# Start of a fused attention and FFN kernel: order of the first loads, the mask by a scan, and batch 0's copies and v factors on other engines

## The chip, the core and the metric

The kernel runs on one core of one Trainium2 chip. The core has five engines with instruction queues of their own: TensorE (PE in the profile), VectorE (DVE), ScalarE (ACT), GpSimd (POOL) and SyncE (SP), and 16 DMA engines that they share. The metric is the device time of one execution in microseconds (us); of several runs the median is taken. Lower is better.

## What is computed

For 8 batches of 8 heads with 576 positions of 64 values, causal attention with a decay: the bias of query i on key j is the difference of a running sum of max(s, 0). Its output, 4608 tokens of 512 values, goes through an RMS norm and a SwiGLU FFN with 1536 hidden columns.

```python
scores = scale * np.matmul(q, k.transpose(0, 1, 3, 2))
cum = np.cumsum(np.maximum(s, 0.0), axis=-1)
bias = -(cum[:, :, :, None] - cum[:, :, None, :])
scores = np.where(causal, -1000000000.0, scores + np.minimum(bias, 0.0))
attn = softmax(scores)                       # over the keys
x = np.matmul(attn, v)                       # to [4608, 512]
xn = x / np.sqrt(np.mean(x * x, axis=-1, keepdims=True) + 1e-06) * rms_g
g = xn @ w_gate
out = (g * sigmoid(g) * (xn @ w_val)) @ w_out
```

(The last lines are put together from the reference's two functions.)

## The kernel before

**Stages.** The kernel works in nine rounds (`for c in range(NCH)`, line 823). Round c computes the FFN of 512 tokens (gate and value products in `ffn1_group`, line 721; output product in `ffn2`, line 740), and beside it prepares and computes the attention of batch c + 1. Batch 0 has no FFN to stand beside: its loads, its preparation and most of its attention (lines 768 to 815) run alone at the start. This stretch is where the change lies.

**The planner.** No order is written by hand. Each instruction is handed to the class `Plan` (line 76) with its engine, an estimated duration in us, a key (lower is more urgent), and for loads two lags and a transfer time. `schedule` (line 140) plays the program through with these estimates: for each engine it takes the most urgent instruction that would be ready, and so fixes the order of every engine's queue. On the chip each engine then works through its queue in that order, and each instruction waits for the data it needs. An estimate is thus no time on the chip, but it decides who stands ahead of whom. `R.after` adds a dependence, `R.order` only an order of starts. Where the plan has TensorE idle in the first 24 us, it fills the gap with dummy products on the tile `still`, "spins" (line 861)[...]. A GpSimd load waits until the load eight before it on that queue has landed (`LANES`, line 83).

**Loads of the start.** GpSimd issues the loads of the start, in one order (`R.order(*loads)`, line 820): K and Q of the first 256 positions of batch 0 (`kqa`), two blocks of v of 128 positions, K and Q of the other 320 positions (`kqb`, the "second part"), the other three blocks of v, then gate and value weights in three pieces each, K and Q of batch 1 in two pieces each, half of the output weights, v of batch 1, and the other half. These loads turn fp32 into bf16 for K, Q and weights; K of batch 0 lands beside Q in the tile `q_nat`, and those of batch 1 in `k_nat`.

**Constants.** `ident_bf` is a 128x128 identity in bf16 for transposes on TensorE. Before, GpSimd makes it with `make_identity` (a memset and a select) between the loads `kqa` and the first v. `tri` is a 128x128 mask: 0 where the query is not before the key, -30000 elsewhere. GpSimd makes it with a memset and a select (lines 781 to 783). TensorE adds it to batch 0's diagonal score blocks as a product of `ident_bf` and `tri`. `ident_F` is the identity in fp32, copied by VectorE (line 784).

**Decay.** `decay` (line 516) turns s into factors: max with 0, a scan over 576 positions, an exp on ScalarE, a transpose on TensorE into a PSUM tile (`wP`), and a copy of that to SBUF in bf16 (`wT`). The bias becomes a factor on each row of v: `prep_v` (line 498) multiplies a block of v by it. For batch 0 all five blocks are done by VectorE from `wP`; for later batches GpSimd does it from `wT`. A dependence puts batch 0's last three blocks behind `norms[3]`, the fourth head pair's division by the softmax sum.

**Transposes of K and Q.** `prep_transpose` (line 460) takes one of four head pairs: TensorE transposes K and Q into two PSUM banks, VectorE copies K to `KT`, ScalarE copies Q to `QT`. Batch 0 goes through it twice, part 0 for the first 256 positions and part 1 for the rest.

**Attention of batch 0.** `attention` (line 689) works in two halves of four units (a unit is a head pair): scores on TensorE (`unit_scores`), exp on ScalarE, then the product with v on TensorE (`unit_av`) and the division on VectorE. The second half needs part 1 of K and Q, all five v blocks, and also the "near" scores between the halves (`near_scores`). For each block of 128 tokens the squares are summed (`att_square`), GpSimd makes the norm's factor alpha (`att_alpha`, two instructions), VectorE or ScalarE scales, TensorE transposes, and VectorE writes `xnT` (`att_out`), which the FFN reads. The first FFN group needs `xnT` of token blocks 0 and 1 and the first pieces of both weights.

Of the kernel before, what the change touches and what calls it, by code (L numbers as in the profile page):

```python
# [270 lines left out]
def kernel(  # L271
# [12 lines left out]
    nc = tc.nc  # L284
    fp32 = mybir.dt.float32
# [3 lines left out]
    ALU = mybir.AluOpType  # L289
    AX = mybir.AxisListType  # L290

    B, H, S, D = q.shape
# [4 lines left out]
    NB = 5  # L297
# [19 lines left out]
    pers = ctx.enter_context(tc.tile_pool(name="pers", bufs=1))  # L317
# [3 lines left out]

    ident_bf = pers.tile([128, 128], bf16, name="ident_bf")
    still = pers.tile([128, 256], bf16, name="still")
    tri = pers.tile([128, 128], bf16, name="tri")
    ident_F = pers.tile([128, 128], fp32, name="ident_F")
    ident_f = ident_F[0:64, 0:64]
# [5 lines left out]
    s_all = pers.tile([BH, S], fp32, name="s_all")  # L332
# [4 lines left out]
    wT = pers.tile([128, NB, BH], bf16, name="wT")  # L337
# [38 lines left out]
    R = Plan(banks)  # L376
# [3 lines left out]
    def real(a):  # L380
        return a.get(banks) if isinstance(a, View) else a

    def I(eng, method, us, key=None, kind=None, dma=0.0, lags=(1.2, 1.2), **kw):
        outs = [kw[n] for n in ("out", "accum_out") if n in kw]
        ins = [a for n, a in kw.items()
               if n not in ("out", "accum_out") and isinstance(a, (bass.AP, View))]
        f = getattr(ENG[eng], method)
        o = R.add(eng, us, lambda: f(**{n: real(a) for n, a in kw.items()}), outs, ins, key=key,  # L388
                  lat=LAT[eng], kind=kind, dma=dma,
                  name=outs[0].bank.name if isinstance(outs[0], View) else outs[0].name)  # L390
        o.lags = lags
        return o

    def fill(eng, ap, value, us, key=None):
        f = ENG[eng].memset
        return R.add(eng, us, lambda: f(ap, value), [ap], [], key=key, lat=LAT[eng], name=ap.name)

    def mms(us, items, key=None):
        def emit():
            for out, lhsT, rhs, st, sp, tr in items:  # L400
                out = real(out)
                if tr:
                    nc.tensor.matmul(out, lhsT=lhsT, rhs=rhs, is_transpose=True, start=st, stop=sp)  # L403
                else:
                    nc.tensor.matmul(out, lhsT=lhsT, rhs=rhs, start=st, stop=sp)  # L405
        o = R.add("pe", us, emit, [i[0] for i in items],
                  [i[1] for i in items] + [i[2] for i in items], key=key, lat=0.22,
                  name=items[0][0].bank.name)
        o.n_mm = len(items)
        return o  # L410
# [8 lines left out]
    def bank(group, cap):  # L419
        return View(Bank(group, group, cap))  # L420
# [4 lines left out]
    def lay(b, dt, pattern=None, n=None, **sizes):  # L425
        a = b if dt == fp32 else b.bitcast(dt)
        a = a[:, 0:n] if n else a
        return a.rearrange(pattern, **sizes) if pattern else a


    def load_runs(b, which, h0, h1, key, part=0):
        c0, c1 = PARTS[part] if b == 0 else (0, KC)
        p0 = KP * which
        us = ((1.5, 1.6)[part] * (h1 - h0) / 8) if b == 0 else 2.85 * (h1 - h0) / 8
        return I("pool", "dma_start", 0.7, key=key, dma=us, lags=(0.95, 1.1),
                 out=raw[b][part][p0 : p0 + KP, h0:h1, :, :].rearrange("p h c d -> p h (c d)"),
                 in_=(k, q)[which][b, h0:h1, KP * c0 : KP * c1, :].rearrange(
                     "h (p c) d -> p h (c d)", c=c1 - c0))
# [7 lines left out]
    def load_rows(dst, src, b, eng, key):  # L446
        return [load_row(dst, src, b, sc, eng, key) for sc in range(NB)]
# [12 lines left out]
    def prep_transpose(b, hp, key, part=0):  # L460
        c0, c1 = PARTS[part] if b == 0 else (0, KC)
        n, t0 = c1 - c0, KP * c0
        t = [lay(bank("kq", 4), bf16, "p (c t) -> p c t", n=KP * n, c=n) for w in range(2)]
        mm = mms(0.1 + 0.025 * n if b == 0 else 0.34,
            [(t[w][64 * j : 64 * j + 64, c, :], raw[b][part][KP * w : KP * w + KP, 2 * hp + j, c, :],
              ident_bf[KP * w : KP * w + KP, KP * w : KP * w + KP], c == 0, c == n - 1, True)
             for c in range(n) for j in range(2) for w in range(2)], key=key)
        for w, dst in enumerate((KT, QT)):
            o = dst[b % 2][:, hp, t0 : t0 + KP * n].rearrange("p (t c) -> p t c", c=n)
            i = t[w].rearrange("p c t -> p t c")  # L470
            if w == 0:
                I("dve", "tensor_copy", 0.12 + 0.062 * n, key=key, out=o, in_=i)
            else:
                I("act", "activation", 0.18 + 0.045 * n, key=key, out=o, in_=i, func=AF.Copy)
        return mm
# [22 lines left out]

    def prep_v(b, sc, eng, key):
        n = 128 if sc < 4 else 64  # L500
        wb = (wP if b == 0 else wT)[0:n, sc, b * H : (b + 1) * H]
        return I(eng, "tensor_tensor", 1.0 if eng == "pool" else 0.62, key=key,
          out=vw[b % 2][0:n, sc, :, 0:64], in0=v_nat[b % len(v_nat)][0:n, sc, :, :],
          in1=wb.unsqueeze(2).to_broadcast([n, H, D]), op=ALU.mult)

    def prep_w(b, eng, key):
        for n, c0, c1 in ((128, 0, 4), (64, 4, 5)):
            o = vw[b % 2][0:n, c0:c1, :, 64:65]
            i = wT[0:n, c0:c1, b * H : (b + 1) * H].unsqueeze(3)
            if eng == "act":  # L510
                I("act", "activation", 0.25, key=key, out=o, in_=i, func=AF.Copy)
            else:
                I(eng, "tensor_copy", 0.25, key=key, out=o, in_=i)


    def decay(key):
        I("dve", "tensor_scalar", 0.5, key=key, out=s_all, in0=s_all, scalar1=0.0, scalar2=None,
          op0=ALU.max)
        I("dve", "tensor_tensor_scan", 1.3, key=key, out=cum, data0=ones[:, 0:1].to_broadcast([BH, S]), data1=s_all, initial=0.0,
          op0=ALU.mult, op1=ALU.add)  # L520
        I("dve", "tensor_scalar", 0.1, key=key, out=half, in0=cum[:, S - 1 : S], scalar1=-0.5,
          scalar2=None, op0=ALU.mult)
        I("act", "activation", 0.7, key=key, kind="exp", out=w_row[:, 0:S], in_=cum, func=AF.Exp,
          bias=half, scale=1.0)
        tp = lay(bank("w", 1), fp32, "p (c b) -> p c b", n=NB * BH, c=NB)
        mms(0.6, [(tp[:, sc, :], w_row[:, sc * 128 : (sc + 1) * 128], ident_f, sc == 0,
                   sc == NB - 1, True) for sc in range(NB)], key=key)
        I("dve", "tensor_copy", 0.42, key=key, out=wT, in_=tp)
        return tp
# [210 lines left out]
    def ffn2(c, key, step):  # L740
# [24 lines left out]
    STEP = PER / 144  # L765


    I("sp", "dma_start", 0.5, key=-100, dma=0.5, out=s_all, in_=s.rearrange("b h s -> (b h) s"))
    I("sp", "dma_start", 0.5, key=-90, dma=0.1, out=g4,
      in_=moe_rms_g.rearrange("(cc p) -> cc p", p=128))  # L770
    fill("dve", still, 0.0, 0.1, key=-101)
# [2 lines left out]
    def ident(t, key):  # L774
        R.add("pool", 0.5, lambda: make_identity(nc, t), [t], [], key=key, lat=0.06).n_pool = 2

    kqa = [load_runs(0, w, h, h + 8, -100) for h in range(0, H, 8) for w in range(2)]
    ident(ident_bf, -99.5)
    kqb = [load_runs(0, w, h, h + 8, -92, part=1) for h in (0,) for w in range(2)]
    v0 = load_rows(v_nat[0], v, 0, "pool", -94)  # L780
    R.add("pool", 0.25, lambda: nc.gpsimd.memset(tri, 0.0), [tri], [], key=-99.3, lat=0.06)
    I("pool", "affine_select", 0.35, key=-99.3, out=tri, in_=tri, pattern=[[1, 128]],
      compare_op=ALU.is_ge, fill=-30000.0, base=0, channel_multiplier=-1)
    I("dve", "tensor_copy", 0.15, key=-93.7, out=ident_F, in_=ident_bf)
    wl = []
    for i, (lo, hi) in enumerate(zip(WL, WL[1:])):
# [1 line left out]
            wl.append(load_w(w, lo * 128, hi * 128, -93 + 0.1 * i))  # L788
    dec = len(R.ops)
    wP = decay(-95)  # L790
    fills = []
    for t in KT:
        fills.append(fill("dve", t[:, :, S : NB * 128], 0.0, 0.17, key=-90))
# [10 lines left out]
    o = mms(0.1, [(gp_[:, 0:CC], g4, ident_F[0:CC, 0:CC], True, True, True)], key=-75)  # L804
    R.after(o, kqt[HP - 1])
    I("dve", "tensor_copy", 0.1, key=-75, out=g_sb, in_=gp_[:, 0:CC])
    prep_w(0, "act", -70)
    vops = [prep_v(0, sc, "dve", -70 if sc < 2 else -62) for sc in range(NB)]
    norms = attention(0, -78, 3, 4)
    for o in vops[2:]:  # L810
        R.after(o, norms[3])
# [2 lines left out]
    for o in R.ops[n0:]:  # L814
# [7 lines left out]
           in_=moe_rms_g.unsqueeze(0).to_broadcast([128, DM]))  # L822
    for c in range(NCH):
# [4 lines left out]
        b = c + 1  # L828
        if b < B:
# [12 lines left out]
            vops = [prep_v(b, sc, "pool", K - 8 + sc) for sc in range(NB)]  # L842
        if b + 1 < B:
            n = b + 1
            K2 = K - 14 + LEAD
            for sc in range(NB):
                for dst, src in ((k_nat, k), (q_nat, q)):
                    o = load_row(dst, src, n, sc, "sp", K2 + sc)
# [186 lines left out]
```

## Time and profile before

| what | us |
|---|---|
| median of 7 runs | 354.05 |
| lowest and highest of them | 352.5 and 354.64 |
| the profiled execution | 353.3 |
| its span, first to last instruction | 351.6 |
| TensorE busy in the span | 341.3 (97%) |
| K and Q of the first part: issued | 1.33 and 2.23 |
| first block of v: issued | 4.23 |
| K and Q of the second part: issued | 6.04 and 6.72 |
| first FFN product starts | 24.33 |

The profile is of one execution. Its span is shorter than its time by 1.7 us, which lie before the first and after the last instruction that the profile shows. Times within it count from the first instruction. A row of the timeline gives start, length, engine, line, operation, the tiles written and read (without their number in the ring for PSUM and for groups), and in brackets how long the engine had been idle before, and what ended it. Most instructions are recorded on lines 388, 403 and 405, the helpers that issue them, so tiles tell them apart. "POOL ... DMA_DIRECT2D" is GpSimd's work of issuing a load; the data land later. The chain of waits is followed back from the last instruction, at each step to whatever released it.

### The profile page before, as it was taken

How to read it: one execution, taken by the hardware profiler on the slowest of the kernel's cores; microseconds unless marked ns; L12 is line 12 of the kernel's file. 1: busy time of each engine (PE TensorE's matmuls, PEld its weight loads, DVE VectorE, ACT ScalarE, POOL GpSimd, SP SyncE). 2: the span in 40 equal slices, each digit the busy share in tenths (PEclk: the TensorE clock that was granted, in tenths of full speed). 3: DMA queues.
4: the chain of work that ended last, by engine and by line, in shares of the span. 5: the costliest groups of instructions: out<-in, count | busy, mean ns of one | idle time of the engine just before them, and what ended most of it. 6: DMA issues, size and time to landing. Idle time of an engine off the chain costs nothing.

```text
span 351.6 us, 8062 instructions
## 1 busy us (share of the span) xinstructions
PE 341.3 (97%) x3037; PEld 209.4 (60%) x3037; DVE 254.8 (72%) x497; ACT 228.9 (65%) x467; POOL 127.0 (36%) x201
## 2 busy tenths in 40 slices
PE   7799999999999999999999999999999999999994
PEld 5579775788479765886544554455455444444443
DVE  5878868698568994989499958996787557707730
ACT  2769999785767986857695668666988433223321
POOL 8754294501481339113921293029325100000000
PEclk9899999999999999999999999999999999999999
DMA  7999998997898886997967896777631130020012
GB/s 140 209 209 207 261 198 185 204 219 172 194 145 230 139 187 119 228 157 178 147 173 182 190 173 156 209 176 140 171 77 33 58 102 0 1 91 30 0 36 93
DMA packets 140550, 51.16 MB, mean 145 GB/s; under 512 B 127316, under 2 KB 135256, under 8 KB 140504
## 3 DMA queue, kind: packets, MB, share of 16 engines
q1 hardware_dynamic: 131832, 41.13, 52.9%
q0 software_dynamic: 8672, 9.44, 14.8%
q8 instruction: 26, 0.43, 0.5%
q14 instruction: 20, 0.16, 0.2%
HBM read 38.16 MB, written 9.44 MB: 135 GB/s over the span
## 4 chain that ended last, share of the span: by engine, by line
PE 93%; DMA 2%; POOL 1%; DVE 1%; issue 1%; ACT 0%; POOLq 0%; DVEq 0%; ACTq 0%
PE psc L405 14%; PE psb L405 12%; PE psf L405 12%; PE psd L405 11%; PE psa L405 11%; PE psg L405 11%; PE pse L405 10%; PE psh L405 10%; DMA q_nat<-in_q_dram 2%; POOL q_nat L388 1%; POOL v_nata L388 1%; PE psa L403 0%; PE psb L862 0%; PE psf L403 0%; PE psh L403 0%
## 5 line engine op out<-in xcount | busy, mean ns | idle before, releaser
L405 PEld LDWEIGHTS <-wg_sb 128*128 128x128 bf16 x624 | 60.0, 98 | 32.5 <-issue 0.4
L405 PEld LDWEIGHTS <-wv_sb 128*128 128x128 bf16 x624 | 59.7, 98 | 32.8 <-issue 1.8
L405 PEld LDWEIGHTS <-Hs 128*128 128x128 bf16 x444 | 41.1, 98 | 42.0 <-DVE Hs L388 0.2
L388 POOL TENSOR_SCALAR_AFFINE_SELECT Eb<-Eb 128x512 bf16<-128x512 bf16 x7 | 4.5, 639 | 78.5 <-ACT Eb L388 78.5
L405 PE MATMUL psc<-wout_sb,Hs 128*128 128x512 bf16 x96 | 23.7, 379 | 0.0
L388 DVE SCALAR_TENSOR_TENSOR x_blkb<-x_blkb,alb,gB 128x512 bf16<-128x512 bf16 x15 | 12.7, 892 | 11.0 <-POOL alb L388 11.0
L405 PE MATMUL psf<-xnT,wg_sb 128*128 128x256 bf16 (+1 forms) x116 | 20.6, 313 | 0.0
L388 POOL TENSOR_TENSOR vwb<-v_nata,wT 128x512 bf16<-128x512 f32 (+1 forms) x20 | 20.3, 1040 | 0.0
L388 ACT ACTIVATE sq_scr<-x_blkb 128x512 bf16<-128x512 bf16 x20 | 12.7, 633 | 10.0 <-DVE x_blkb L388 9.6
L405 PE MATMUL psb<-wout_sb,Hs 128*128 128x512 bf16 (+1 forms) x84 | 19.0, 364 | 0.0
L405 PE MATMUL psa<-xnT,wv_sb 128*128 128x256 bf16 (+1 forms) x108 | 18.6, 308 | 0.0
L388 ACT ACTIVATE sq_scr<-x_blka 128x512 bf16<-128x512 bf16 x18 | 11.4, 632 | 9.6 <-DVE x_blka L388 9.4
L405 PE MATMUL psg<-xnT,wv_sb 128*128 128x256 bf16 (+1 forms) x108 | 17.6, 300 | 0.0
L388 ACT ACTIVATE sq_scr<-q_bf 128x1024 bf16<-128x1024 bf16 (+1 forms) x18 | 16.4, 914 | 0.2
L405 PE MATMUL psd<-wout_sb,Hs 128*128 128x512 bf16 (+1 forms) x72 | 16.4, 361 | 0.0
L388 ACT ACTIVATE sq_scr<-k_bf 128x1024 bf16<-128x1024 bf16 (+1 forms) x18 | 16.3, 906 | 0.0
L388 DVE CAST k_bf<-k_nat 128x512 bf16<-128x512 f32 (+1 forms) x30 | 16.1, 537 | 0.0
L388 POOL TENSOR_TENSOR vwa<-v_nata,wT 128x512 bf16<-128x512 f32 (+1 forms) x15 | 15.4, 1052 | 1.1 <-DMA v_nata<-in_v_dram 1.0
L405 PE MATMUL psc<-xnT,wv_sb 128*128 128x256 bf16 (+1 forms) x84 | 15.5, 318 | 0.3 <-DVE u_sbc L388 0.3
L388 POOL TENSOR_SCALAR_AFFINE_SELECT Ef<-Ef 128x512 bf16<-128x512 bf16 (+1 forms) x14 | 7.1, 527 | 23.9 <-ACT Ef L388 23.9
L405 PE MATMUL psb<-xnT,wg_sb 128*128 128x256 bf16 (+1 forms) x92 | 15.5, 305 | 0.0
L388 DVE CAST q_bf<-q_nat 128x512 bf16<-128x512 f32 (+1 forms) x30 | 15.3, 510 | 0.0
(475 smaller groups left out, 874.2 us busy)
## 6 DMA issues: line engine op xcount, KB each, us to landing
v_nata<-in_v_dram SPq DMA_DIRECT2D x24, 256.0 KB, 4.2
k_nat<-in_k_dram SPq DMA_DIRECT2D x24, 256.0 KB, 3.2
q_nat<-in_q_dram SPq DMA_DIRECT2D x24, 256.0 KB, 3.7
out_dram<-osba SPq DMA_DIRECT2D x12, 256.0 KB, 2.3
out_dram<-osbb SPq DMA_DIRECT2D x12, 256.0 KB, 2.4
out_dram<-osbc SPq DMA_DIRECT2D x11, 256.0 KB, 3.0
v_nata<-in_v_dram POOLq DMA_DIRECT2D x8, 256.0 KB, 9.9
wout_sb<-in_moe_w_out_dram POOLq DMA_DIRECT2D x2, 768.0 KB, 15.8
```

Of the source, the lines that this page charges most:

```text
L388: o = R.add(eng, us, lambda: f(**{n: real(a) for n, a in kw.items()}), outs, ins, key=key, lat=LAT[eng], kind=kind, dma=dma, name=outs[0]. ...
L405: nc.tensor.matmul(out, lhsT=lhsT, rhs=rhs, start=st, stop=sp)
```

## The change

- GpSimd issues the first two v loads straight behind `kqa`. The identity's memset is now VectorE's, and its select stands behind the second v load (`R.order(v0[1], o)`).
- The mask is no longer made by GpSimd. VectorE makes it from the identity: a scan along each row, with a column of ones (`one`) as factor, gives 1 from the diagonal on and 0 before it; then subtract 1 and multiply by 30000. Both instructions are put behind the decay's `half`.
- The planner's lags for the load of s are 0.8 and 0.8 where they were 1.2 and 1.2.
- Blocks 2, 3 and 4 of batch 0's v get their factors on GpSimd, from `wT`; blocks 0 and 1 stay on VectorE, from `wP`.
- In the second part, VectorE copies Q of head pairs 2 and 3; ScalarE keeps those of 0 and 1.

```diff
@@ -321,6 +321,7 @@
     still = pers.tile([128, 256], bf16, name="still")
+    one = pers.tile([128, 1], fp32, name="one")
@@ -468,7 +469,7 @@
-            if w == 0:
+            if w == 0 or part and hp in (2,3,):
                 I("dve", "tensor_copy", 0.12 + 0.062 * n, key=key, out=o, in_=i)
             else:
                 I("act", "activation", 0.18 + 0.045 * n, key=key, out=o, in_=i, func=AF.Copy)
@@ -498,7 +499,7 @@
-        wb = (wP if b == 0 else wT)[0:n, sc, b * H : (b + 1) * H]
+        wb = (wP if eng == "dve" else wT)[0:n, sc, b * H : (b + 1) * H]
@@ -765,7 +766,7 @@
-    I("sp", "dma_start", 0.5, key=-100, dma=0.5, out=s_all, in_=s.rearrange("b h s -> (b h) s"))
+    I("sp", "dma_start", 0.5, key=-100, dma=0.5, lags=(0.8, 0.8), out=s_all, in_=s.rearrange("b h s -> (b h) s"))
@@ -775,12 +776,13 @@
     kqa = [load_runs(0, w, h, h + 8, -100) for h in range(0, H, 8) for w in range(2)]
-    ident(ident_bf, -99.5)
     kqb = [load_runs(0, w, h, h + 8, -92, part=1) for h in (0,) for w in range(2)]
     v0 = load_rows(v_nat[0], v, 0, "pool", -94)
-    R.add("pool", 0.25, lambda: nc.gpsimd.memset(tri, 0.0), [tri], [], key=-99.3, lat=0.06)
-    I("pool", "affine_select", 0.35, key=-99.3, out=tri, in_=tri, pattern=[[1, 128]],
-      compare_op=ALU.is_ge, fill=-30000.0, base=0, channel_multiplier=-1)
+    fill("dve", ident_bf, 0.0, 0.1, key=-100)
+    fill("dve", one, 1.0, 0.06, key=-100)
+    o = I("pool", "affine_select", 0.35, key=-99.5, out=ident_bf, in_=ident_bf,
+          pattern=[[-1, 128]], compare_op=ALU.not_equal, fill=1.0, base=0, channel_multiplier=1)
+    R.order(v0[1], o)
@@ -788,6 +790,13 @@
     wP = decay(-95)
+    n = len(R.ops)
+    I("dve", "tensor_tensor_scan", 0.35, key=-89, out=tri, data0=one.to_broadcast([128, 128]),
+      data1=ident_bf, initial=0.0, op0=ALU.mult, op1=ALU.add)
+    I("dve", "tensor_scalar", 0.15, key=-89, out=tri, in0=tri, scalar1=-1.0, scalar2=30000.0,
+      op0=ALU.add, op1=ALU.mult)
+    for o in R.ops[n:]:
+        R.after(o, R.ops[dec + 2])
@@ -805,7 +814,7 @@
-    vops = [prep_v(0, sc, "dve", -70 if sc < 2 else -62) for sc in range(NB)]
+    vops = [prep_v(0, sc, "dve" if sc < 2 else "pool", -70 if sc < 2 else -62) for sc in range(NB)]
```

## The prediction, made before the result was known

> **What bounds the kernel now.** I read the page first, then the chain that ended last, the timeline of the first 40 us, and stretches. The page says that TensorE is the bound over the span as a whole:
>
> ```profile
> PE 341.3 (97%) x3037; PEld 209.4 (60%) x3037; DVE 254.8 (72%) x497; ACT 228.9 (65%) x467; POOL 127.0 (36%) x201
> ```
>
> All that the change touches runs before the first FFN group, so the question is when that group starts. The chain of waits over 0 to 40 us (start, length, what) shows what comes ahead of it:
>
> ```profile
> 4.28 1.78 POOL v_nata L388 x2
> 6.06 0.67 POOL q_nat L388
> 6.72 7.59 DMA q_nat<-in_q_dram
> ...
> 17.04 1.40 PE psb L862 x6
> ...
> 23.02 0.38 PE psc L405 x12
> ...
> 24.49 0.87 PE psb L405 x8
> ```
>
> The last is the first FFN group; from there the chain is TensorE almost without a break, so a microsecond gained before 24.3 us moves the end by a microsecond, if later loads keep up. Ahead of it stands Q of the second part: issued at 6.72, landed at 14.31. GpSimd could issue it only after two v loads, and these only after it had made identity and mask (2.90 to 4.28). TensorE idles for it, and then runs at half clock (columns: busy us of each engine, granted clock, DMA share, GB/s):
>
> ```profile
> 5.14:8.55 3.41, 2.36 (x50) 1.81 (x51) 2.35 (x10) 1.16 (x2) 3.41 (x6) 1.00 1.19 235
> 11.96:15.38 3.42, 1.76 (x64) 1.28 (x62) 2.20 (x11) 1.77 (x6) 2.08 (x5) 1.00 1.16 260
> 15.38:18.79 3.41, 3.41 (x44) 2.14 (x44) 2.69 (x7) 2.20 (x6) 2.37 (x5) 0.50 1.35 203
> ```
>
> In the second part the timeline shows ScalarE as the last link: two Q copies stand among its exps, and it has two stalls of 0.8 us:
>
> ```profile
> 16.40 0.60 ACT L388 ACTIVATE Ee<-psf 128x512 bf16<-128x512 f32 x1 [0.84 <-PE psf L405]
> 17.98 0.44 ACT L388 ACTIVATE QTa<-psh 128x320 bf16<-128x320 bf16 x1
> 19.23 0.60 ACT L388 ACTIVATE Ef<-psb 128x512 bf16<-128x512 f32 x1 [0.81 <-PE psb L405]
> 20.20 0.44 ACT L388 ACTIVATE QTa<-psd 128x320 bf16<-128x320 bf16 x1
> 23.35 0.62 ACT L388 ACTIVATE Eh<-psg 128x512 bf16<-128x512 f32 x1
> ```
>
> Its last exp ends at 23.97; the last attention-times-v group starts at 23.96 to 24.00. The other feeder, xnT of token blocks 0 and 1, is ready at 22.46 + 0.67 = 23.13.
>
> [...] 0.50 for exactly 3.41 us, after a window that was 52% busy (1.76 of 3.42); after one that was 69% busy (2.36 of 3.41) it stayed full. [...] GpSimd's loads landed in the order of issue (K 6.2, Q 7.6, v 8.3 and 9.7, K 12.5, Q 14.3). So v loads issued earlier should not hold up K and Q that are ahead of them. [...] The trace shows 1.35 us for the 64x576 scan against 0.45 for the tensor_scalar of that shape.
>
> **Part 1, v loads ahead of the identity.** GpSimd spends 2.90 to 4.23 = 1.33 us on four instructions between Q's load and v. Three go away (both memsets, the mask's select); the identity's select (0.29) comes after the two v loads. So v is issued 1.33 earlier, and the second part's K and Q 1.33 - 0.29 = 1.04 earlier (Q at about 5.7). That the landing moves by as much is not given: the DMA engines are busy most of the time. What can be saved is the dip when v has drained and K has not started (0.5 us slices):
>
> ```profile
> 7.50:8.00 0.50, 0.29 (x16) 0.25 (x16) 0.00 (x0) 0.00 (x0) 0.50 (x1) 1.00 1.04 270
> 8.00:8.50 0.50, 0.50 (x17) 0.43 (x18) 0.42 (x1) 0.39 (x1) 0.50 (x2) 1.00 0.78 164
> 8.50:9.00 0.50, 0.50 (x36) 0.36 (x36) 0.48 (x2) 0.18 (x1) 0.50 (x1) 1.00 0.80 104
> 9.00:9.50 0.50, 0.50 (x20) 0.34 (x20) 0.50 (x3) 0.50 (x4) 0.50 (x2) 1.00 0.96 141
> 9.50:10.00 0.50, 0.50 (x21) 0.34 (x17) 0.42 (x2) 0.50 (x3) 0.50 (x2) 1.00 1.30 175
> ```
>
> Against a share of about 1.2 from 9.5 to 13 us, the slices 0.78, 0.80 and 0.96 lack 0.42 + 0.40 + 0.24 = 1.06; times 0.5 over 1.2 that is 0.44 us. I take **0.5**; bounds 0 [...] and 1.04. The identity is then ready at about 5.1; its first user waits for K until 6.45, so the delay is covered by 1.3 us.
>
> **Part 2, mask by scan, fills on VectorE.** Added there: memsets of the identity (0.11 to 0.17, like its neighbours) and of the column of ones (0.06), in the idle time before 3.54; the scan, by the 3-column scan at 0.12 and the 576-column one at 1.35: 0.12 + 125 x 2.15 ns = 0.39; the tensor_scalar about 0.2. ident_F's copy (0.23) moves behind the decay scan; the relu starts some 0.1 earlier. They sit behind the fills, which end at 7.3; the first K copy starts at 8.07 after an idle 0.75. 0.39 + 0.2 + 0.23 - 0.1 = 0.72 fits; overrun at most 0.2, and the first half of batch 0 has a 1.4 us wait for Q behind it (VectorE idle until 14.82). The mask's first use is at 9.06. Cost **0**. The lags of the s load alter only the planner's due times: 0.
>
> **Part 3, three v factors to GpSimd, two Q copies to VectorE.** VectorE sheds 3 x 0.68 = 2.04 us and takes 2 x 0.49 (the 128x320 K copy's price) = 0.98. ScalarE sheds the copies at 17.98 and 20.20, 2 x 0.44 busy, about 0.38 each start to start: **0.75**, on the path because its last exp is. GpSimd takes 3 x 1.04 = 3.1 us, after the fourth norm of the first half (15.9) and the v landings (16.1 and later). Queued behind them are the issues of batch 1's K and Q (17.26 to 20.87) and the alpha pair (18.58 to 19.58). Later issues cost nothing as long as the queue is fed: the weights ahead of them land as late as 16.52 + 15.9 = 32.4. The factors are needed by 22.86; three of them end at 20 to 21. But alpha feeds xnT: one factor ahead of it costs nothing, three bring xnT to about 22.9. I give back **0.3** for that.
>
> **Part 4, the half clock.** With Q 0.5 earlier, TensorE's busy time in 11.96 to 15.38 goes from 1.76 to about 2.3 (67%), near the 69% that kept the clock full. Half clock cost 0.44 on the scores (1.23 us from 15.37 against 0.79 for the same unit at 22.13) and 0.7 on the six spins (1.40 instead of 6 x 0.12). VectorE's earlier K copies bind in its place, so of 1.14 I take **0.8**, bounds 0 (window falls low again) and 1.14.
>
> **Sum.** 0.5 + 0.75 + 0.8 - 0.3 = 1.75: the first FFN group at 22.6 instead of 24.33. Does the rest keep up? The wv columns for group two land at 12.80 + 12.2 = 25.0 (24.5 shifted) and are first used at 26.95; batch 1's Q lands at 17.87 + 17.5 = 35.4 and its transposes start at 37.10. These slacks, 1.95 and 1.7, plus 0.5 cap the gain at about 2.2; at 1.75 they hold. I leave the gain at **1.7** after rounding down for new stalls. Profiled execution: 351.6 of span + 1.7 around it = 353.3; less 1.7 = 351.6. The median of the runs, 354.05, lies 0.75 above it; so **352.3**.
>
> **Rivals.** **A, the rebalancing is covered** (0.24): the planner's new order keeps TensorE waiting for copies, and only arrival and a little of the clock count, 0.7: 353.35. For it: VectorE holds K copies behind norm and square (15.48 to 16.64). Against: ScalarE really is last. **B, GpSimd becomes the bound** (0.14): all three factors ahead of alpha, or the dip only moves; gain about 1.0: 353.05. For it: GpSimd waits in order; against: alpha has the more urgent key. **C, slower** (0.13): the half clock moves instead of going. If TensorE is busy less than 52 to 69% (1.8 to 2.4 us) of the window 18.79 to 22.20, because fewer spins are planned in a shorter second part, half clock falls on 22.20 to 25.61. Then the 1.47 us of attention-times-v take 1.4 more and the FFN to 25.6 loses about 0.9, less 0.6 of arrival: +1.7, so 355.75. For it: three engines are emptier there; against: the window is 3.14 of 3.41 busy now.
>
> **Numbers.** Forecast 0.49. A measurement of this kernel can tell about 0.3% (1.06 us) from no change: faster is below 353.0, slower above 355.1. Faster: 0.45 of the forecast, 0.05 of A, 0.07 of B = 0.57; slower: C and a little of A = 0.14; same 0.29. Range: low end the 2.2 cap and scatter among runs, 351.2; high end takes in A and B with scatter, 354.7. The forecast's own range is 351.6 to 353.0.
>
> **What would show it.** Q landing near 13.8 (step 1); no copy of VectorE later than 8.3 for the scan (2); ScalarE without the copies at 18 and 20 and alpha before 19.5 (3); no 0.50 stretch after 15 us (4); the first FFN group near 22.6 and no TensorE wait up to 55 us (sum). It is wrong if Q still lands at 14.3, if xnT is later than the last exp, or if half clock lies over the FFN.

## The result, and the profile after

The changed kernel is slower: a median of 356.35 us in 15 runs (353.38 to 360.39) against 353.78 us in 36 runs of the kernel before, a ratio of 1.0068 with a 95% interval of [1.0044, 1.0092]. The longest run, over 1.5% above the shortest, is left out of the ratio. The profiled execution took 358.59 us with a span of 356.8, near the top of its runs; a second profile of the same text, taken later, has 356.66 and 355.0. Both are used below.

The page's first line, to be held against that of before. TensorE's busy time is 1.8 us longer and the span 5.2 us: most of the loss is TensorE standing still.

```profile
PE 343.1 (96%) x3034; PEld 210.2 (59%) x3034; DVE 255.7 (72%) x500; ACT 228.1 (64%) x465; POOL 129.7 (36%) x201
```

The chain of waits over 0 to 40 us (start, length, what):

```profile
2.90 1.82 POOL v_nata L389 x2
4.72 0.07 POOLq L389 x2
4.79 0.79 POOL ident_bf L389
5.58 0.66 POOL q_nat L389
6.25 7.29 DMA q_nat<-in_q_dram
...
19.12 0.20 POOL ala L389
19.32 0.07 issue
19.39 0.74 POOL ala L389
20.16 1.15 DVE x_blka L389
21.31 0.05 issue
21.35 0.40 PE psb L404 x4
...
25.05 1.19 PE psg L406 x8
```

Q of the second part lands at 6.25 + 7.29 = 13.54 instead of 14.31, as was hoped. But GpSimd's alpha, which was not on the chain before, is on it now, and the first FFN group starts at 24.86 instead of 24.33. GpSimd's queue shows why alpha is late (the last column is the idle time ahead of an instruction and what ended it):

```profile
16.23 0.74 POOL L389 DMA_DIRECT2D wv_sb<-in_moe_w_val_dram  x1 [1.67 <-DMA v_nata<-in_v_dram]
16.98 2.05 POOL L389 TENSOR_TENSOR vwa<-v_nata,wT 128x512 bf16<-128x512 f32 x2
19.12 0.19 POOL L389 TENSOR_SCALAR ala<-ssa 128x2 f32<-128x2 f32 x1
```

A weight load, the 15th load of this queue, waits 1.67 us for a block of v, the 7th (0.95 us before), two factors follow it, and alpha comes behind both. Until alpha is there, the transposes of x can't run, and in TensorE's queue they stand ahead of the last scores. ScalarE's last exp therefore waits 2.35 us for its scores:

```profile
22.41 0.60 ACT L389 ACTIVATE Eh<-psh 128x512 bf16<-128x512 f32 x1 [2.35 <-PE psh L406]
```

The stretches (TensorE, weight loads, VectorE, ScalarE, GpSimd busy; clock; DMA share; GB/s) show the half clock gone from 15.3 to 18.7 and come back at 22.1, after a window in which TensorE was busy for 1.02 of 3.41 us:

```profile
15.31:18.73 3.42, 3.36 (x82) 2.27 (x79) 2.56 (x7) 3.40 (x8) 2.48 (x3) 1.00 1.45 193
18.73:22.14 3.41, 1.02 (x16) 0.62 (x15) 1.75 (x3) 1.33 (x3) 3.24 (x6) 1.00 1.25 207
22.14:25.55 3.41, 3.41 (x50) 3.21 (x49) 2.35 (x7) 1.09 (x2) 2.34 (x4) 0.50 1.18 209
```

That looks like the whole story, and it isn't. The output products of the first round start 1.04 us later than before, those of rounds two to four 1.2 us later, and those from round five on 5.6 us later. Between them lies a wait of 2.5 us of TensorE, from 55 us on by far its longest (total, times, longest in us), and half clock comes with it, from 179.15 to 182.56: the four products behind the wait took 1.84 us, four like them at full clock 1.03. Wait and half clock together make up nearly all of the 4.4 us.

```profile
PE psc L406 <- DMA xnT<-x_blka: 2.5, 1, 2.5
PE psa L406 <- DVE x_blkb L389: 0.4, 1, 0.4
```

```profile
179.09 1.84 PE L406 MATMUL psc<-xnT,wg_sb 128*128 128x512 bf16 x4 [2.51 <-DMA xnT<-x_blka]
```

In the trace of before the longest wait of that stretch is 0.4 us, and none is for a DMA:

```profile
PE psh L405 <- DVE x_blkb L388: 0.4, 1, 0.4
```

The view of the DMA queues differs too, although nothing in the change seems to touch most of what it counts. It gives packets, megabytes and the time that the packets took as a share of 16 engines' span; SyncE's loads and transposes are in q1. Before, and then after:

```profile
q1 hardware_dynamic: 131832, 41.13, 52.9%
...
v_nata<-in_v_dram SPq DMA_DIRECT2D x24, 256.0 KB, 4.2
```

```profile
q1 hardware_dynamic: 131832, 41.13, 59.2%
...
v_nata<-in_v_dram SPq DMA_DIRECT2D x24, 256.0 KB, 5.1
```

The same packets and bytes took a good tenth more time; a v load of SyncE lands after a median of 5.1 us, where it was 4.2.

### The profile page after: what moved, and what is told of

Its sections match the earlier page's. It is cut to its first block, busy times and chain, and to the rows that moved or that the text cites. A ratio compares the mean times of both kernels' runs of the same rounds, so it can differ in the third digit from the quotient of the medians.

```text
span 356.8 us, 8055 instructions
## 1 busy us (share of the span) xinstructions
PE 343.1 (96%) x3034; PEld 210.2 (59%) x3034; DVE 255.7 (72%) x500; ACT 228.1 (64%) x465; POOL 129.7 (36%) x201
## 3 DMA queue, kind: packets, MB, share of 16 engines
q1 hardware_dynamic: 131832, 41.13, 59.2%
## 4 chain that ended last, share of the span: by engine, by line
PE 90%; DMA 3%; POOL 2%; DVE 2%; SPq 1%; ACT 1%; issue 1%; POOLq 0%; DVEq 0%; ACTq 0%
PE psg L406 13%; PE psc L406 12%; PE psd L406 11%; PE psh L406 11%; PE psf L406 11%; PE psa L406 10%; PE pse L406 10%; PE psb L406 10%; DMA q_nat<-in_q_dram 2%; SPq L389 1%; DMA xnT<-x_blka 1%; POOL q_nat L389 1%; PE psb L404 1%; POOL v_nata L389 1%; DVE x_blka L389 0%
## 5 line engine op out<-in xcount | busy, mean ns | idle before, releaser
L406 PE MATMUL psg<-wout_sb,Hs 128*128 128x512 bf16 x96 | 23.3, 379 | 0.0
L406 PE MATMUL psd<-xnT,wg_sb 128*128 128x256 bf16 (+1 forms) x124 | 21.7, 310 | 0.0
L389 POOL TENSOR_TENSOR vwa<-v_nata,wT 128x512 bf16<-128x512 f32 (+1 forms) x18 | 18.8, 1062 | 3.3 <-DMA v_nata<-in_v_dram 3.1
L406 PE MATMUL psc<-wout_sb,Hs 128*128 128x512 bf16 (+1 forms) x84 | 19.3, 364 | 0.0
L406 PE MATMUL psb<-xnT,wv_sb 128*128 128x256 bf16 (+1 forms) x100 | 17.5, 311 | 0.0
L406 PE MATMUL psf<-xnT,wv_sb 128*128 128x256 bf16 (+1 forms) x100 | 16.5, 303 | 0.0
L406 PE MATMUL psh<-wout_sb,Hs 128*128 128x512 bf16 (+1 forms) x72 | 16.4, 361 | 0.0
L406 PE MATMUL psc<-xnT,wg_sb 128*128 128x256 bf16 (+1 forms) x68 | 13.2, 330 | 2.5 <-DMA xnT<-x_blka 2.5
L406 PE MATMUL psa<-xnT,wv_sb 128*128 128x256 bf16 (+1 forms) x80 | 15.3, 328 | 0.0
```

## The experiments

Each row is set against runs of the kernel before, timed beside it. The first row is the result above; the others were timed in four sessions, in which the kernel before had medians of 353.56, 353.40, 353.43 and 353.05 us (rows 2 to 5, 6 to 9, 10 to 13, and 14 to 16). Not all sessions ran on the same chip, so rows of different sessions are compared by their ratios. The verdicts rest on the ratio, which need not be exactly that of the medians.

| kernel | median us | ratio and interval |
|---|---|---|
| changed kernel | 356.35 | 1.0068 [1.0044, 1.0092] |
| changed, factors on VectorE | 354.36 | 1.0033 [1.0014, 1.0053] |
| before, factors on GpSimd (order redrawn) | 358.15 | 1.0121 [1.0091, 1.0151] |
| changed, alpha first (order redrawn) | 356.54 | 1.0083 [1.0055, 1.0112] |
| changed, factors and Q copies as before | 354.72 | 1.0037 [1.0021, 1.0054] |
| before, factors on GpSimd, order kept | 354.88 | 1.0042 [1.0023, 1.0061] |
| changed, alpha first, order kept | 354.42 | 1.0010 [0.9985, 1.0035] |
| before, order redrawn only | 357.21 | 1.0103 [1.0068, 1.0138] |
| changed, factors on VectorE, alpha ahead of batch 1 | 354.22 | 1.0038 [1.0013, 1.0063] |
| changed, tile of ones padded | 353.60 | 0.9994 [0.9973, 1.0015] |
| before, shifted by 32 bytes | 354.60 | 1.0030 [1.0008, 1.0053] |
| changed, alpha first, padded | 352.36 | 0.9980 [0.9956, 1.0004] |
| changed, factors on VectorE, padded | 352.82 | 0.9980 [0.9960, 0.9999] |
| before, shifted by 64 bytes | 353.84 | 1.0019 [0.9999, 1.0039] |
| before, shifted by 128 bytes | 353.41 | 1.0006 [0.9980, 1.0032] |
| changed, factors on VectorE, alpha ahead, padded | 352.26 | 0.9976 [0.9958, 0.9995] |

### First: parts undone

**Factors back on VectorE.**

```diff
-    vops = [prep_v(0, sc, "dve" if sc < 2 else "pool", -70 if sc < 2 else -62) for sc in range(NB)]
+    vops = [prep_v(0, sc, "dve", -70 if sc < 2 else -62) for sc in range(NB)]
```

> The changed kernel, but with all five of batch 0's v factors on VectorE as before. Theory (the factors hold GpSimd's alpha back, and TensorE stands behind alpha): alpha starts near 17.2 instead of 19.1, TensorE has no wait of 2.4 us for the scaled x, no half clock lies over 22 to 25.5 us, the first FFN group starts at 22.5 to 23.0, and the time is 1 to 2 us under the kernel before. Rival one (VectorE's Q copies are to blame): the wait stays, time 355.5 to 357. Rival two (a later stage upset by the new order): start early, but time still above 355.

Ratio 1.0033: half of the loss is gone, but the kernel isn't faster than before. In the profile the first FFN group starts at 22.76, as expected, so the start alone doesn't decide the time. Alpha ran from 19.04 to 20.05, for GpSimd waited 1.50 us for v ahead of a weight load, and 0.49 for it again ahead of K of batch 1.

**Factors alone, on the kernel before.**

```diff
-        wb = (wP if b == 0 else wT)[0:n, sc, b * H : (b + 1) * H]
+        wb = (wP if eng == "dve" else wT)[0:n, sc, b * H : (b + 1) * H]
...
-    vops = [prep_v(0, sc, "dve", -70 if sc < 2 else -62) for sc in range(NB)]
+    vops = [prep_v(0, sc, "dve" if sc < 2 else "pool", -70 if sc < 2 else -62) for sc in range(NB)]
```

> The kernel before, with three of batch 0's v factors moved to GpSimd and nothing else. Theory: GpSimd makes two factors (2.05 us) ahead of alpha, which starts near 19.4 instead of 18.6; VectorE's scaling of x is slowed by the third factor as in the changed kernel (1.40 instead of 0.61 for two); the first FFN group starts 1 to 1.5 us later than 24.3; time 355 to 356. Rivals: 353 to 354.5, because the harm comes from the Q copies or the loads.

358.15, slower than the whole change. In its profile the distance of the output products from those of before grew from 1.75 to over 5 us, so most of it was not lost at the start.

**Alpha first, on the changed kernel.**

```diff
     for o in vops[2:]:
-        R.after(o, norms[3])
+        R.after(o, norms[3], alphas[0, 0])
...
     R.order(*loads)
+    R.after(kq1[0], alphas[0, 0])
```

> The changed kernel with one order added: GpSimd's three factors, and the first load of batch 1, stand behind alpha of token blocks 0 and 1. Theory: alpha starts near 17.1 and ends near 18.1, factors 18.2 to 21.2, first FFN group near 22.5 to 23, no half clock after 18 us; time 352 to 353. Rival one (the factors cost as such, wherever they stand): 355 or more. Rival two (a later stage): start early, time above 355.

The first output products started 0.83 us before those of before, and yet the kernel took 356.54: it lost 3 us and more between rounds two and six.

**Loads and mask alone**, the changed kernel with factors and Q copies as before:

```diff
-            if w == 0 or part and hp in (2,3,):
+            if w == 0:
...
-    vops = [prep_v(0, sc, "dve" if sc < 2 else "pool", -70 if sc < 2 else -62) for sc in range(NB)]
+    vops = [prep_v(0, sc, "dve", -70 if sc < 2 else -62) for sc in range(NB)]
```

> The changed kernel with factors and Q copies both as before, so that only the order of the loads, the mask by the scan and the lags remain. Theory: Q of the second part lands at 13.5 as in the changed kernel, the window at 12 to 15.4 us keeps the clock full, first FFN group near 23.2; time 352.5 to 353.3. Rival (the earlier loads or the scan do harm): 355 or more.

Ratio 1.0037, the same as with the Q copies on VectorE (1.0033). What was taken to be the harmless part of the change costs about 1.3 us by itself.

### Second: the planner's order held still

Two of these results were hard to reconcile, so the instruction queues of the programs were compared engine by engine. From batch 1 on the changed kernel, and the two that put its factors back, have the queues of the kernel before but for a few places. The factors-alone and the alpha-first kernel don't: there VectorE, ScalarE, GpSimd and SyncE stand in another order on some 270 places. The estimates decide who goes first, and a small difference at the start draws the rest anew. Small changes of one estimate bring the old order back, or change it and nothing else.

```diff
 before, order redrawn only
-    I("sp", "dma_start", 0.5, key=-100, dma=0.5, out=s_all, in_=s.rearrange("b h s -> (b h) s"))
+    I("sp", "dma_start", 0.5, key=-100, dma=0.5, lags=(1.1, 1.1), out=s_all, in_=s.rearrange("b h s -> (b h) s"))
 factors alone, order kept (beside the edit above)
-        return I(eng, "tensor_tensor", 1.0 if eng == "pool" else 0.62, key=key,
+        return I(eng, "tensor_tensor", 1.15 if eng == "pool" and b == 0 else 1.0 if eng == "pool" else 0.62, key=key,
 alpha first, order kept (beside the edit above)
+        return I(eng, "tensor_tensor", 0.85 if eng == "pool" and b == 0 else 1.0 if eng == "pool" else 0.62, key=key,
```

> The kernel before, with nothing but the planner's two lags for the load of s at 1.1 instead of 1.2. No instruction is added, taken away or given to another engine; the order from batch 1 on becomes, but for 9 places, the one that the factors-only and the first alpha-first run had. If that order costs time by itself: 356 to 357, with waits of TensorE for x_blkb of 1 us and more at 87 to 130 us. If it doesn't: 353.6 to 354.0.

> The kernel before with the three v factors on GpSimd, and the planner's estimate of such a factor raised from 1.0 to 1.15 us. With 1.0 (the factors-only run, 358.15) the planner also drew another order of all engines from batch 1 on, on some 270 places; with 1.15 the order from batch 1 on is that of the kernel before. Theory one (alpha stands behind two factors in GpSimd's queue, the scale of x and the transposes come late): the first FFN group 1.2 to 2 us later, and that is all: 355.0 to 355.7. Theory two (of the 4.4 us of the factors-only run most came from the order drawn anew): 354 to 355.5 as well, but the starts of the output products stay at a constant distance from those before, where they went from +1.75 to +5.8. Rival (the order is of no account, GpSimd's load is what costs): 358 again.

> The changed kernel with alpha ahead of the three factors and of batch 1's loads in GpSimd's queue, as in the alpha-first run (356.54), but with the estimate of batch 0's factors lowered to 0.85, so that the order from batch 1 on is that of the kernels before and after. Theory one (alpha's place is the whole loss): alpha from about 17.1 to 18.1, no idle TensorE of over 1 us between 18.7 and 22, first FFN group at 22.5 to 23, and 353.0 to 354.0, below the changed kernel by 2.4 or more. Theory two (alpha's place costs 1.2 and the rest of the loss is later, in SyncE's queue or in transfers): 355. Rival (GpSimd's factors themselves, wherever they stand): 356.4.

The redraw alone costs 1.0103; the factors-alone kernel lost about as much beyond its order-kept twin (1.0121 against 1.0042). Its waits of TensorE from 55 us on are led by one that the trace of before has at 0.4 us:

```profile
PE psd L405 <- DVE x_blkb L388: 1.9, 2, 1.1
PE psd L405 <- POOL Eh L388: 0.4, 1, 0.4
```

So the first factors-alone and alpha-first runs tell nothing of their edits. With the order kept, the factors on GpSimd cost 1.0042 on the kernel before, some 1.5 us. That is less than theory one had; the range and the constant distance are those of theory two. But in that one profile the output products come 0.6 us before those of before, so where the cost lies isn't shown. The clock is a candidate: the 22 runs of this kernel had a mean granted clock of 0.9895, the 55 of the kernel before 0.9931. By an estimate from these two, if TensorE bounds throughout, that is 0.0036 of 354 us, or 1.3 us. On the changed kernel, alpha ahead of the factors takes the ratio from 1.0068 to 1.0010: its place is worth 1.5 us there by the medians and 2 by the ratios. Alpha ran from 18.66 to 19.67, not from 17.1: the sums of squares came only then.

**Alpha ahead of batch 1's loads, with the factors on VectorE:**

```diff
     R.order(*loads)
+    R.after(kq1[0], alphas[0, 0])
```

> The changed kernel with all five factors on VectorE (the factors-back run, 354.36) and batch 1's first load put behind alpha, so that alpha no longer stands behind two issues that wait for v to land; the order from batch 1 on is unchanged. Theory one (alpha's place decides the start): alpha ends at about 18.2 instead of 20.05, TensorE's wait of 0.71 us for x goes, and the time falls by 0.7 to 1.2, to 353.2 to 353.7. Rival (the scores and exps of the second part bind in its place, or the later load of batch 1 costs what alpha gains): 354.4.

Alpha came 1.3 us earlier (to 18.78) and TensorE's wait of 0.7 us for x went, as theory one has it; the time stayed (1.0038 against 1.0033), as the rival has it. Something kept these kernels 1 us above the kernel before, whatever was done to their start.

### Third: addresses

In the view of the DMA queues the runs fall in two groups: q1 has 59 to 62% of the span in the changed kernel, with the factors back, with alpha first, with loads and mask alone; and 51 to 53% in the kernel before, with the factors alone, with the redraw. The first group has a tile that the second hasn't, `one`. It takes 4 bytes in each partition, which the allocation rounds up to 32, and it is allocated ahead of nearly everything. The addresses in the built programs show it: in the kernel before, `k_nat`, `q_nat`, `v_nata`, `k_bf` and `q_bf` start on multiples of 256 bytes (`k_nat` at 99,840 = 390 x 256); in the changed one each starts 32 bytes further on. Not all tiles are on such a boundary before: `xnT` starts 128 bytes past one, and `KT` and `QT` 192.

```diff
 padded
-    one = pers.tile([128, 1], fp32, name="one")
+    one = pers.tile([128, 64], fp32, name="one")[:, 0:1]
 before, shifted (1, 16 or 32 columns for 32, 64 or 128 bytes)
     still = pers.tile([128, 256], bf16, name="still")
+    shift = pers.tile([128, 1], fp32, name="shift")
```

The padded kernels with alpha first, and with the factors on VectorE, have the edits shown above for these beside the padding.

> The changed kernel with the tile of ones made 256 bytes wide in each partition instead of 4; only its first column is used. The 4 bytes, which the allocation rounds up to 32, push every tile behind it 32 bytes on; 256 bytes leave each tile where it was relative to a boundary of 256. All engines' orders are those of the changed kernel. In the runs so far each kernel that has the small tile shows the loads of SyncE's queue at 59 to 62% of the DMA engines' span, each one without it at 50 to 53%, for the same bytes. Theory one (the shift by 32 bytes slows the DMA engines, and this is the part of the loss that no change of order took away): the share falls to 52 to 54%, and the time by 1.5 to 2.5, to 353.9 to 354.9; what stays above 353.5 is alpha behind the factors. Rival (the share comes from the new order of the first loads, or costs nothing): 59% and 356.3, or 53% and 356.3.

> The kernel before with one more tile of 4 bytes in each partition, allocated at the same place as the ones of the change and used by no instruction. No instruction and no order changes; all tiles behind it lie 32 bytes further on. Theory one (the shift slows the DMA engines): SyncE's loads at 59 to 61% of the span instead of 53%, v loads of SyncE at a median of 5 us to landing instead of 4.2, and 354.9 to 356.0 in place of 353.5. Rival (addresses are of no account): 353.5 and 53%.

> The changed kernel with both repairs: alpha ahead of the factors in GpSimd's queue with the order from batch 1 on kept (354.42 alone), and the tile of ones at 256 bytes. If the two causes are separate and add up: 352.0 to 352.9, faster than the kernel before by 0.5 to 1.5, with SyncE's loads at 53%. If alpha's place and the shift are one and the same delay seen twice: 354.4.

> The changed kernel with all five factors on VectorE (354.36 alone) and the tile of ones at 256 bytes. What is left of the change is then the order of the first loads, the mask by the scan and the two Q copies. Theory one (the shift cost this kernel 1.5 to 2.5): 351.9 to 352.9, near the 352.3 that was predicted for the whole change. Rival (the early loads and the scan cost time by themselves): 354.4.

What was foretold comes in kind in all four. Two sizes miss: the padded kernel gains 0.3 us more than theory one's range (353.60 under 353.9), and the shift costs 0.3 less (354.60 under 354.9). The shift alone, of a tile that nothing uses, makes the kernel before slower (1.0030) and gives it the changed kernel's mark, the waits for xnT. The DMA queues and TensorE's waits from 55 us on, in the shifted kernel:

```profile
q1 hardware_dynamic: 131832, 41.13, 60.0%
...
v_nata<-in_v_dram SPq DMA_DIRECT2D x24, 256.0 KB, 5.4
```

```profile
PE psb L406 <- DMA xnT<-x_blka: 1.1, 1, 1.1
PE psh L406 <- DMA xnT<-x_blkb: 0.9, 1, 0.9
```

That the engines' own accesses are slower at the new addresses can be ruled out: in the shifted kernel and in the kernel before TensorE was busy for 340.2 and 341.3 us, VectorE for 254.3 and 254.8, ScalarE for 228.4 and 228.9, and GpSimd for 127.0 in both.

Padding the tile, with every queue as it was, takes the changed kernel from 1.0068 to 0.9994, and its DMA queues and waits back to those of before:

```profile
q1 hardware_dynamic: 131832, 41.13, 52.2%
...
v_nata<-in_v_dram SPq DMA_DIRECT2D x24, 256.0 KB, 4.3
```

```profile
PE psa L406 <- DVE x_blkb L389: 0.4, 1, 0.4
```

Its GpSimd queue can be compared with that of the changed kernel above. v landed in time, the weight load waited for nothing, and both factors were done before alpha's sums of squares were ready:

```profile
15.13 0.74 POOL L389 DMA_DIRECT2D wv_sb<-in_moe_w_val_dram  x1
15.88 2.05 POOL L389 TENSOR_TENSOR vwa<-v_nata,wT 128x512 bf16<-128x512 f32 x2
18.68 0.19 POOL L389 TENSOR_SCALAR ala<-ssa 128x2 f32<-128x2 f32 x1 [0.75 <-ACT Ef L389]
```

The view names `Ef` as what ended alpha's wait, but alpha reads the sums of squares, and of these VectorE's came last, at 18.42 + 0.08 = 18.50. The square for it stood beside the two factors and took 2.28 us; before, with no factor on GpSimd, it took 0.69:

```profile
15.94 0.69 DVE L388 SCALAR_TENSOR_TENSOR sq_scr<-x_blka 128x512 bf16<-128x512 bf16 x1
```

```profile
16.20 2.28 DVE L389 SCALAR_TENSOR_TENSOR sq_scr<-x_blka 128x512 bf16<-128x512 bf16 x1
18.42 0.08 DVE L389 DVE_READ_ACCUMULATOR sq_scr<-x_blka 128x1 f32 x1
```

The same is seen in every trace in which this square meets the factors: 2.42 us in the changed kernel's second profile and 2.74 with the factors alone, and in all three it ends some 0.55 us after the second factor does. In the other traces it took 0.69. So the factors on GpSimd delay alpha in two ways: they stand ahead of it in the queue, and they hold up the square that it needs.

### Fourth: which boundary, and the changed kernel again

The two wider shifts, the padding together with factors on VectorE and alpha ahead of batch 1's loads, and the changed kernel with no edit:

> The kernel before with an unused tile of 64 bytes in each partition at the place of the ones, so that all tiles behind it lie 64 bytes further on. Theory one (a load writes pieces of 256 bytes[...]): as with 32 bytes, SyncE's loads at 59 to 61% of the span, the 256-byte packets at a mean of 22 ns, about 354.6. Theory two (only multiples of 64 bytes matter): 53%, 19 ns, 353.5.

> The kernel before with an unused tile of 128 bytes, all tiles behind it 128 bytes further on. Theory one (a boundary of 256): 59 to 61%, 22 ns, about 354.6. Theory two (64 or 128 is enough): 53%, 19 ns, 353.5.

> The changed kernel with the factors on VectorE, alpha ahead of batch 1's loads on GpSimd, and the tile of ones at 256 bytes: the two best versions put together. With the factors on VectorE and the small tile, alpha's place was worth 0.14 (354.36 against 354.22). Theory one (with aligned tiles v lands early and GpSimd waits for nothing ahead of alpha, so its place is of no account): 352.6 to 353.0, as with the factors back and the tile padded (352.82). Rival (alpha's place is worth a further 0.5 or more): 352.0 to 352.3.

> The changed kernel once more, for a second profile. Theory one (the late landing of v is a matter of addresses and comes again): the issue of the third piece of wv waits over 1 us for v and comes at about 16.2, the factors start at about 17, alpha ends at about 20, TensorE idles over 1 us ahead of the transposes of x; SyncE's loads at 59% or more. [...] Rival (a single late landing): issue at 15.1 to 15.5 and alpha at 18.7 to 19.7, as with the tile padded.

Shifts by 64 and 128 bytes leave q1 at 59.1% and 58.1%: a multiple of 64 or 128 isn't enough for the DMA queue. A cost in time isn't shown for these two: 1.0019 and 1.0006, with intervals that hold 1, where theory one had 354.6. At 64 bytes TensorE waited 1.0 and 0.9 us for xnT, at 128 bytes 0.5. The packets of 256 bytes in q1 took 19.3 ns in the mean before, 22.4 shifted by 32, 21.9 by 64 and 21.6 by 128, and 19.2 padded. Most kept their time: 18 ns or less for 97% of them before and for 71% shifted by 32. Of the packets in GpSimd's queue, shifted by 32 against before, those of 640 to 1536 bytes changed by under 3%, those of 512 bytes went from 61.2 to 66.4 ns, and those of 4096 bytes from 208 to 276.

The changed kernel's second profile repeats the share of q1 and the waits for xnT, and not the rest:

| profile | third wv piece issued | alpha done | first FFN group | half clock from | waits for xnT | q1 |
|---|---|---|---|---|---|---|
| before | 16.52 | 19.58 | 24.33 | 15.38 | none | 52.9% |
| changed | 16.23 | 20.12 | 24.86 | 22.14 and 179.15 | 2.5 | 59.2% |
| changed again | 16.80 | 21.36 | 24.86 | 15.10 | 1.1 and 1.0 | 59.7% |
| changed, padded | 15.13 | 19.69 | 23.18 | 14.89 | none | 52.2% |
| alpha first, padded | 16.05 | 19.02 | 23.64 | none | none | 51.2% |
| factors on VectorE, padded | 15.18 | 19.01 | 23.09 | 15.25 | none | 51.5% |
| factors on VectorE, alpha ahead, padded | 15.16 | 18.66 | 22.58 | none | none | 52.9% |

With 356.66 us it is as slow as the others, but the half clock lies at 15.10, and TensorE's 2.4 us of idle time ahead of the transposes are not there; it waited 1.0 us for a Q copy of VectorE instead. The weight load waited 0.62 us for v, not over 1 as expected. Alpha was late all the same, because the square met the factors:

```profile
17.56 2.04 POOL L389 TENSOR_TENSOR vwa<-v_nata,wT 128x512 bf16<-128x512 f32 x2
20.36 0.19 POOL L389 TENSOR_SCALAR ala<-ssa 128x2 f32<-128x2 f32 x1 [0.75 <-DVE sq_scr L389]
```

The last row is the fastest kernel of the study, 0.9976 [0.9958, 0.9995], so 0.2% below the kernel before, which is at the limit of what can be told. Its 352.26 lies in the rival's range, but the kernel before was faster in the runs it was compared with too (353.05 for 353.43). By the ratio it doesn't differ measurably from the same kernel without alpha's move (0.9980), as theory one has it: with aligned tiles and the factors on VectorE, alpha's place is of little account.

## Why the prediction was wrong

**The step that failed** is part 2, "Cost **0**". It priced the column of ones by its memset of 0.06 us. It never asked what its 4 bytes do to the tiles behind it. Undone by itself, this takes away the loss: 1.0068 to 0.9994, some 2.6 us. On the kernel before the same shift costs 1.0030, some 1.1 us. The three other pairs that differ by the padding alone point the same way (0.9980 for 1.0033, 0.9980 for 1.0010, 0.9976 for 1.0038). The five give 0.0030 to 0.0074, each to about 0.003, so that the price is greater in the changed kernel isn't clear of the noise. Its first profile has a reason that would fit, three factors and alpha behind a load that waits for v; its second has another.

The rest of part 2 held where it counts: the scan took 0.37 us and the first K copy started at 8.21, though the subtraction took 0.66 where 0.2 was said. That the lags cost 0 was luck. The reason given, that they alter only due times, is refuted by the redraw: on the kernel before, a lag of 1.1 instead of 1.2 costs 1.0103, because due times help decide the order.

The runs show the boundary: each of the three shifts off 256 slows the 256-byte packets in the mean, from 19.3 ns to 22.4, 21.9 and 21.6, by 16% at 32 bytes, and with the tile padded to 256 bytes they took 19.2. They don't show how it costs time: 71% of the packets shifted by 32 took 18 ns or less, as 97% did before, so the mean rests on the others, and why these took longer stays open.

**Part 1** said Q 0.5 us earlier, with bounds 0 and 1.04. The issue came only 0.47 earlier instead of 1.04, mostly because the identity's select took 0.79 us where it had taken 0.29, and the landings scatter: 13.54 and 15.15 in the two profiles of the changed kernel, 14.11 to 14.45 in the padded ones, 14.31 before. The gain is 0.2 at most in the aligned kernels, near the lower bound.

**Part 3** gave ScalarE's copies 0.75. Copies on VectorE against copies on ScalarE, other things equal and both with the small tile, measured 354.36 against 354.72, ratios 1.0033 and 1.0037: nothing that can be told from zero. It gave back 0.3 for the factors. On GpSimd they cost 1.0042 alone, 1.0068 for 1.0033 in the changed kernel, and 0.9994 for 0.9980 when padded, where the intervals overlap: 0.5 to 1.5 us, mis-sized even in the sign of the part's sum. One reason is in the traces: a factor holds up VectorE, which the prediction put at nothing. The square took 2.28 to 2.74 us instead of 0.69 beside two factors, and the two scales of x up to 1.40 instead of 0.61 beside one and 2.18 beside three. The square and the scales read x from SBUF, while VectorE's copies from PSUM beside the factors kept their 0.48 us; the factor itself kept its 1.03 to 1.09. What the two engines wait for in each other isn't shown. "Alpha before 19.5" failed in both profiles of the changed kernel (done at 20.12 and 21.36).

**Part 4** took 0.8 for a half clock that goes. On the whole it doesn't: over all runs the mean granted clock was 0.9930 before, 0.9939 after and 0.9935 padded. Where the half clock falls, or whether it comes at all, differs from one execution to the next of the same text (22.14 and 15.10 above). The prediction read one execution's window as a property of the kernel. These means also show that the clock isn't the loss.

**The sum** assumed that a gain ahead of 24.3 us reaches the end. In the padded kernels it does: the output products keep their distance to within 0.2 us over all nine rounds. In most of the shifted ones it doesn't: from round one to nine the changed kernel loses a further 4.6 us (3.0 in its second profile) and the kernel before, shifted by 32 bytes, 3.1: there SyncE's v loads land after a median of 5.1, 5.2 and 5.4 us instead of 4.2, and TensorE waits for xnT, for 2.5, for 1.1 and 1.0, and for 1.1 and 0.9 us. The one with the factors on VectorE and alpha ahead of batch 1 keeps its distance to 0.2 us in its profile. The prediction looked for slack among GpSimd's loads alone. Padded, the change gives 0.9994, not the forecast's 1.7 us: parts 1, 3 and 4 together are worth nothing that can be told either.

**The rivals.** C named 355.75, nearest to the result, and its half clock at 22.2 to 25.6 is there in the first profile. It isn't the cause: the second profile is as slow without it, and the mean clock of all runs isn't lower than before. So C's number came near by luck. B, GpSimd as the bound, describes what the shift made of GpSimd's queue, but not the size. A, a covered rebalancing, comes nearest to what the padded kernel shows. Open stays how the cost of the factors on GpSimd divides among the queue ahead of alpha, the square held up and the clock, and why the select took 0.79 us; neither was tried.

## What to carry to other kernels

A new tile moves all tiles that are allocated behind it: round small ones up to 256 bytes (here that took the ratio from 1.0068 to 0.9994; allocating them last wasn't tried), and compare the share of the DMA queues before anything else when the packets are the same and the time isn't (59.2% against 52.9% here). Where a planner fixes the order from estimates, hold the order still in each experiment, since a lag changed by 0.1 alone cost 1%. Before work moves to GpSimd, look at what VectorE does beside it (here a square of 2.28 to 2.74 us instead of 0.69). Half clock seen in one execution is no property of the kernel until other executions show it (here from 22.14 in one profile of the changed kernel and from 15.10 in the other).

## What the runs showed of the hardware

- The tiles that K, Q and v are loaded into shifted off a 256-byte boundary in SBUF, by 32 bytes: packets of 256 bytes at 22.4 ns in the mean instead of 19.3, and SyncE's queue at 60.0% of the DMA engines' span instead of 52.9%, for equal packets. Multiples of 64 and 128 bytes don't restore it (59.1% and 58.1%).
- A VectorE square of bf16 128x512 (two inputs from SBUF) beside two GpSimd products of 128x512: 2.28, 2.42 and 2.74 us instead of 0.69, ending some 0.55 us after the products each time. Two VectorE scales of that shape: up to 1.40 us beside one product and 2.18 beside three, instead of 0.61. The products took 1.03 to 1.09 each, and VectorE's copies from PSUM beside them 0.48.
